# Two layer-norm weaves, one load and one block of values moved ahead in a fused attention and feed-forward kernel

## The chip, the core and the metric

The kernel runs on one core of one Trainium2 chip. The metric is the time of one execution on the device in microseconds; lower is better. The core has five engines with instruction streams of their own: TensorE (PE; its weight loads are PEld), VectorE (DVE), ScalarE (ACT), GpSimd (POOL) and SyncE (SP), which here issues nearly all DMA transfers.

## The reference

A block of a transformer with conditioned layer norms: an attention with a compressive memory in four segments, and then a bilinear feed-forward part. Sizes: 2048 rows, width 512, 32 heads of 16, segments of 512 rows, inner width 1376, all float32.

```
mod = silu(c) @ w_mod ; sa, ca, ga, sb, cb, gb = 6 rows of 512
h = layernorm(x) * (1 + ca) + sa
q, k, v = heads(h @ wq), heads(h @ wk), heads(h @ wv)
M, z = 0, 0
for s in range(4):                        # segments
    p = softmax(qs ks^T / 4 + mask)       # mask: -1e9 where key > query position
    a_dot = p vs
    a_mem = phi(qs) M / (phi(qs) z + 1e-6)       # phi(t) = t + 1 if t > 0 else exp(t)
    o_s = g * a_mem + (1 - g) * a_dot            # g = sigmoid(beta), one per head
    M, z = M + phi(ks)^T vs, z + sum(phi(ks))
x = x + ga * (o @ wo)
h = layernorm(x) * (1 + cb) + sb
out = x + gb * (((h @ w_gate) * (h @ w_up)) @ w_down)
```

The mask in full: `(ar[:, None] < ar[None, :]) * (-1e9)` over query and key positions.

## The kernel before

**Precision.** Dense products are made of three matmuls: operands are split into a high part (rounded to the fp32r format, names ending in H) and a low remainder (ending in L), and H·H, L·H and H·L are accumulated. Queries and keys are split into three bf16 parts and written to DRAM (`qd`, `kd`), from where `load(u)` reads them back into stacked tiles `qst`, `kst` (96 rows).

**Attention units.** A unit is one segment, one half of a head group: 4 heads. There are 4 segments x 4 head groups x 2 = 32 units. For a unit, five `q_step`s make scores with queries on the partitions; VectorE reduces each to a negated row maximum `nm` (the custom operation at L39, in place in the PSUM tile `q`, followed by a read of its accumulator). The score tiles have two PSUM banks, `lq0` and `lq1`. `n_step` transposes the maxima (`ntp`), rounds them to two bf16 rows (`nt`) and sends these with two small DMAs into rows 96 and 97 of `qst`. Five `k_step`s then make scores with keys on the partitions, maximum already taken off by those rows; ScalarE takes the exponential (`pt`, L289), GpSimd zeroes the masked part (L292). `av_step` multiplies with the values into `tb`, and `t_step` transposes back (`tr`) and scales into `orow`. `load` is L230, the `nt` DMAs L269.

**The loop.** The main loop runs over `v` from -2 to 32, each with five slots. In slot `slot` of turn `v` there are: one `q_step` of unit v+1 or v+2, in slot 1 the four `av_step`s of unit v-1, in slot 4 its `t_step`, then a portion of fill, and one `k_step` of unit v. TensorE's instructions stay in the order in which the program calls them (`MM` and `TP` chain each to the one before). VectorE's do as well from the loop on (`vec.eng = CV`). ScalarE's, GpSimd's and SyncE's instructions are ordered by a scheduler that plans with estimated times; `pin` ties some of them behind the TensorE instruction called last.

**The fill.** Everything else is written as generators. `fill_a` makes values (`a_v`), key and query projections (`a_kq`, PSUM tiles `kps`, `qps`), memory steps (`a_mem`: `mp`, `mz`, `up`) and the layer norms of segments 1 to 3 (`ln`, names beginning with `a`); `fill_b` makes output projections (`wo_op` transposes `op` and splits them into `oH`, `oL`; `wo_mm` multiplies into `wops`), the split of `wo` (`woH`, `woL`) and the norm `lnC` of the feed-forward part (`ctp`, `chf`, `chH`). Each yields the cost of what it has called (0.68 for three matmuls of 128x512, 0.45 for a group of transposes, 0.0 for steps with no TensorE work). `fill(share)` adds share x 5.5 to a credit and draws steps until it is used up; a yielded `False` ends the portion. The shares of the five slots are 0.25, 0, 0.25, 0.25, 0.25. What is left when the last unit is done is run at once, ahead of the feed-forward part, which then runs over four segments with TensorE alone in front.

**The layer norm.** `ln` yields 0.0 after each of four row statistics (`bn_stats` and `bn_aggr` on VectorE, tiles `ast`, `amv`), after the inverse deviation (two ScalarE and five GpSimd operations, `asd`, `ay`), and after each of four applications (`tensor_scalar` on VectorE, L39, on the row tiles `x`). Then come four groups of transposes (`atp`), each followed by a ScalarE scaling (`ahf`, L183), rounding (`ahH`) and a GpSimd remainder (`ahL`, L191). `weave(a, b, at)` runs generator `a` and draws one step of `b` behind those yields of `a` whose number is in `at`; a projection `a_kq` has four such yields. For segments 2 and 3 the norm is woven into the query projection of head group 2 and both projections of group 3; for segment 1 only into both of group 3. What is left of it runs unwoven ahead of the next segment (`yield from lns`).

**Before the loop.** The weights of a head group are loaded raw into a staging buffer (`staged`, tags from the list `stage`) and split by ScalarE and GpSimd. The tag `x` has four buffers; the rows of segment 0 use them first, then the raw weights of head groups 1, 2 and 3, and the rows of segment 1 (`xload`, L459) come behind these. Projections of head groups 0 and 1 and two of four value blocks of segment 0 are made ahead of the loop; two more blocks come as the first fill.

Of the kernel before, what the change touches and what calls it, by code (L numbers as in the profile page):

```python
# [8 lines left out]
F32 = mybir.dt.float32  # L9
# [8 lines left out]
P = 128  # L18
S, D, H, DH, NSEG, L, F = 2048, 512, 32, 16, 4, 512, 1376
# [38 lines left out]
def tile_kernel(ctx, tc, x, wq, wk_, wv, wo, beta, w_gate, w_up, w_down, c, w_mod, out):  # L58
# [4 lines left out]
    def open_pool(**kw):  # L63
        p = tc.tile_pool(**kw)
        return p, p.__enter__()
# [18 lines left out]
    def MM(*a, **k):  # L84
        return pe(nc.tensor.matmul(*a, **k))  # L85
# [12 lines left out]
    def pst(shape, tag, name, dt=F32):  # L98
        tg, n = TAGS[tag]
        return psp.tile(list(shape), dt, tag=tg, name=name, bufs=n)  # L100
# [105 lines left out]
    apool, ap = open_pool(name="ap", bufs=1)  # L206
# [20 lines left out]
    def load(u):  # L227
        s, g, j = u // 8, u // 2 % 4, u % 2
        for t, d in ((kst[u % NB], kd), (qst[u % NB], qd)):
            nc.sync.dma_start(t[0:96].rearrange("p h t -> p (h t)"),  # L230
                              d[s][g].rearrange("r (d h) t -> (r d) (h t)", h=HG)[:, j * HQ * L:(j + 1) * HQ * L])
# [3 lines left out]
    def q_step(u, i):  # L235

        Q, K = qst[u % NB], kst[u % NB]
        if i == 0:
            nms[u] = ap.tile([P, 16], F32, tag="nm", name=f"nm{u}", bufs=2)
        nm = nms[u]  # L240
        for b in range(2):
# [7 lines left out]
            for hh, qb in parts:  # L249
                n = (qb + 1) * P  # L250
                MM(qp[:, c:c + n], Q[0:96, hh, qb * P:(qb + 1) * P], K[0:96, hh, 0:n], start=True, stop=True)
                c += n
# [7 lines left out]
    def n_step(u):  # L260

        Q = qst[u % NB]
        tp = pst([16, P], "tb", f"ntp{u}", F32)
# [4 lines left out]
        for i in range(2):  # L268
            nc.sync.dma_start(Q[96 + i:97 + i].rearrange("p h (q t) -> p (h q) t", t=P), nt[:, i])  # L269

    def k_step(u, i):

        Q, K = qst[u % NB], kst[u % NB]
        kp = psp.tile([P, 2, 512], F32, tag="lk", name=f"k{u}_{i}", bufs=1)

        def mm(b, c, h, kb):
            MM(kp[:, b, c:c + L - kb * P], K[:, h, kb * P:(kb + 1) * P], Q[:, h, kb * P:], start=True, stop=True)

# [164 lines left out]
    papool, pa = open_pool(name="pa", bufs=2, reuse_waits="tile")  # L443
# [3 lines left out]
    def load_mod(i):  # L447
        r = []
        for k in range(KT):
            a = pa.tile([P, 512], F32, tag="x", name=f"wm{i}_{k}", bufs=4)  # L450
            nc.sync.dma_start(a, wm[:, k, i * D:(i + 1) * D])
            r.append(a)
        return r

    def xload(s):
        xt = []
        for t in range(4):
            a = pa.tile([P, D], F32, tag="x", name=f"x{s}_{t}", bufs=4)
            pin(nc.sync.dma_start(a, x[rows(s, t), :]))  # L459
            xt.append(a)  # L460
        return xt
# [37 lines left out]
    def mod_acc(r):  # L499
        for k in range(KT):  # L500
            pin(act.activation(r[k], r[k], AF.Identity, scale=s_c[:, k:k + 1]))
            if k > 0:
                nc.gpsimd.tensor_add(r[0], r[0], r[k])
            yield 0.0
# [44 lines left out]
    def a_ln(s):  # L549
        return ln(pa, pa, xts.pop(s), s, ca_c, sa_c, "a", ("h", 8, 2), s == 0)  # L550

    def weave(a, b, at):

        i = 0
        for w in a:
            yield w
            if w:
                for _ in range(at.count(i)):
                    w = next(b, None)
                    if w or w is False:  # L560
                        yield w
                i += 1

    wH, wL = {}, {}
    stage = [("ph", 3), ("ph", 3), ("ph", 3), ("mem", 1), ("pkr", 1), ("f", 2)] + [("x", 4)] * 6
    nst = [0]

    def staged(nm):
        tg, n = stage[nst[0] % len(stage)]
        nst[0] += 1  # L570
        return pa.tile([P, D], F32, tag=tg, name=f"wr{nm}", bufs=n)

    def load_g(nm, w, g):

        A, V = (CA if g == 0 else act), (CV if g == 0 and nm == "q" else nc.gpsimd)
        raw = staged(f"{nm}{g}")
        hi = wH[nm, g] = pa.tile([P, KT, P], F32R, name=f"w{nm}H{g}", bufs=1)
        lo = wL[nm, g] = pa.tile([P, KT, P], F32R, name=f"w{nm}L{g}", bufs=1)
        pin(nc.sync.dma_start(raw.rearrange("p (k c) -> p k c", c=P),
                              w.rearrange("(k p) n -> p k n", p=P)[:, :, g * P:(g + 1) * P]))  # L580
        yield
        hi, lo = (a.rearrange("p k (d h) -> p k h d", h=HG) for a in (hi, lo))
        raw = raw.rearrange("p (k h d) -> p k h d", k=KT, h=HG)
        pin(A.activation(hi, raw, AF.Copy))
        V.tensor_sub(lo, raw, hi.bitcast(F32))
        yield
# [14 lines left out]
    def a_v(s):  # L601
        hH, hL = hcur[0]
        for t in range(4):
            ps = bank(f"vps{s}_{t}")
            tt = slice(t * P, (t + 1) * P)
            n = 0
            for k in range(KT):
                for a, b in ((hH, wH), (hL, wH), (hH, wL)):
                    MM(ps, a[k][:, tt], b["v", k], start=n == 0, stop=n == 11)
                    n += 1  # L610
                    if n in (3, 6, 9):
                        yield 0.68
            act.activation(vt[s % 2][t][:, 0:H * VS].rearrange("p (h e) -> p h e", e=VS)[:, :, 0:DH],
                                 ps.rearrange("p (h e) -> p h e", e=DH), AF.Copy)
            yield 0.68
# [78 lines left out]
    def drain():  # L694
        while memq:
            w = mem_step()
            if w is not None:
                yield w
# [42 lines left out]
    def a_mod(i, a):  # L741

        if i == 2:
            bcast(a, gab, "gaps")
        elif i == 5:
            bcast(a, gbb, "gbps")
        else:
            cols(a, (sb_c, cb_c)[i - 3], f"mc{i}")
            if i == 4:
                vec.tensor_scalar_add(cb_c, cb_c, 1.0)  # L750
        yield 0.6
# [23 lines left out]
    def fill_a():  # L775
        for w in w2:
            next(w)
        yield from av
        memq.extend((a_mem(0, 0), a_mem(0, 1)))
        lns = None  # L780
        for s in range(NSEG):
            if s > 0:
                hcur[0] = yield from lns
                if s < 3:
                    r = load_mod(2 * s)
            for g in range(2 if s == 0 else 0, NG):
                ws = []
                if s == 0 and g < 3:
                    ws = [load_g(nm, w, g + 1) for nm, w in (("k", wk_), ("q", wq))]
                for w in ws:  # L790
                    next(w)
                K, Q = a_kq(s, g, "k"), a_kq(s, g, "q")
                if g >= 2 and s + 1 < NSEG:
                    if g == 2:
                        xts[s + 1] = xload(s + 1)
                        lns = a_ln(s + 1)
                        if s > 0:
                            Q = weave(Q, lns, (0, 1, 2, 3))
                    else:
                        K = weave(K, lns, (1,) if s > 0 else (0, 1, 2, 3))  # L800
                        Q = weave(Q, lns, (0, 1, 2, 3))
                if g == 1 and 0 < s < 3:
                    acc = mod_acc(r)
                    K, Q = weave(K, acc, (0, 2)), weave(Q, acc, (0, 2))
                if s == NSEG - 1 and g == NG - 1:
                    yield from Q
                    memq.append(a_mem(s, g))
                    yield from K
                    break
                yield from K  # L810
                for w in ws:
                    next(w)
                yield from Q
                if s > 0 and g == 0:
                    while vfree[0] < s:
                        yield None
                    if s < 3:
                        yield from weave(a_v(s), mod_acc(r), (1, 3, 5, 7))
                        yield from a_mod(2 * s, r[0])
                        r = load_mod(2 * s + 1)  # L820
                    else:
                        yield from a_v(s)
                        B["orl"] = wo_load(0, wpool)
                        B["raw"] = [wo_raw(k, wpool, "wor", 2) for k in (0, 1)]
                if g == 1 and 0 < s < 3:
                    yield from a_mod(2 * s + 1, r[0])
                memq.append(a_mem(s, g))
        for w in drain():
            yield w
            yield False  # L830
# [79 lines left out]
    av = a_v(0)  # L910
# [11 lines left out]
    flush()  # L922
    load(1)
    load(2)
    btag[:] = ["ms"]
    vec.eng = CV
    share = (0.25, 0.0, 0.25, 0.25, 0.25)
    for v in range(-2, NQ + 1):
        rate[0] = 5.5
        on, prev = 0 <= v < NQ, 0 <= v - 1 < NQ  # L930
        for slot in range(5):
            i = (slot + 3) % 5
# [53 lines left out]
    for s in range(NSEG):  # L986
# [30 lines left out]
        for i in range(NF):  # L1017
            if i + 1 < NF:
                gate_up(i + 1)
            n = ft[i][1]  # L1020
# [47 lines left out]
```

## Time and profile before

| | |
|---|---|
| median of 3 runs | 920.62 us (920.42 to 922.03) |
| the profiled execution | 918.26 us, span 916.5 us, mean granted TensorE clock 0.989 |
| TensorE busy | 874.2 us (95% of the span), 5083 matmuls |
| VectorE busy | 525.5 us (57%) |
| ScalarE busy | 408.4 us (45%) |
| GpSimd busy | 316.1 us (34%) |
| first score matmul of attention | 41.66 us |

The profile is of one execution. Busy shares are of the whole span; the loop of attention units fills it from about 42 to 527 us, the feed-forward part from 540 us on. The line of an instruction is that of the helper which recorded it: L85 is every matmul of `MM`, L88 every transpose of `TP`, L39 every operation that goes through a chain. So an instruction is told by its tile. A wait names the instruction that ended it, as inferred from semaphores.

### The profile page before, as it was taken

Reading aid. Unit: us, or ns where it says so; the run is one execution under the profiler, and the core shown is the slowest. Engines: PE = TensorE matmul, PEld = TensorE weight load, DVE = VectorE, ACT = ScalarE, POOL = GpSimd, SP = SyncE. Lnnn points to the kernel's source line nnn. Section 1 sums busy time; section 2 is a strip of 40 time slices with the busy share of each in tenths; the row PEclk is TensorE's granted clock in tenths of the full one; section 3 lists DMA queues with packets and bytes.
Section 4 is the critical chain, followed back from the end, with each engine's and each line's share of the span. In section 5 each row is a group of like instructions: output and inputs, shape, how many; then the busy total and the mean of one; then the engine's idle time right before and its main releaser. Section 6 shows DMA issues by size and latency. Waiting matters only on the chain.

```text
span 916.5 us, 14189 instructions
## 1 busy us (share of the span) xinstructions
PE 874.2 (95%) x5083; PEld 623.9 (68%) x5084; DVE 525.5 (57%) x1586; ACT 408.4 (45%) x603; POOL 316.1 (34%) x456
## 2 busy tenths in 40 slices
PE   8898999989999899998997999999999999999998
PEld 5665656656656566565655678887888788878886
DVE  8598778878789787696886326552133213321112
ACT  3667757787577865674546412231112111211111
POOL 4545536566465752665423406540000000000000
PEclk9999999999999999997999999999999999999999
DMA  7774545664455544568551433431101110100011
GB/s 230 223 214 145 156 127 153 194 204 146 135 165 168 177 146 135 177 200 290 163 171 61 134 129 106 113 95 58 46 1 47 46 47 0 46 18 29 1 46 46
DMA packets 86215, 109.81 MB, mean 120 GB/s; under 512 B 9504, under 2 KB 58656, under 8 KB 86144
## 3 DMA queue, kind: packets, MB, share of 16 engines
q1 hardware_dynamic: 86000, 108.89, 38.4%
q8 instruction: 40, 0.66, 0.3%
q14 instruction: 31, 0.25, 0.1%
q10 hardware_dynamic: 144, 0.02, 0.0%
HBM read 67.98 MB, written 40.63 MB: 119 GB/s over the span
## 4 chain that ended last, share of the span: by engine, by line
PE 77%; DVE 14%; ACT 4%; DMA 2%; issue 1%; POOL 1%; SPq 0%; DVEq 0%; ACTq 0%
PE gps L1004 13%; PE acc L1025 13%; PE ups L1004 13%; DVE q L39 7%; PE tb L85 7%; PE k L85 6%; PE q L85 5%; PE wops L85 4%; PE vps L85 3%; PE qps L85 3%; PE kps L85 3%; ACT pt L289 2%; DVE nm L39 1%; PE tr L88 1%; PE wups L85 1%
## 5 line engine op out<-in xcount | busy, mean ns | idle before, releaser
L39 DVE CUSTOM_DVE_ANT_0 q<-q,cmask 128x384 f32<-128x384 f32 (+3 forms) x512 | 245.9, 507 | 61.6 <-PE q L85 53.4
L289 ACT ACTIVATE pt<-k 128x1024 f32<-128x1024 f32 x160 | 163.7, 1023 | 75.4 <-PE k L85 72.3
L292 POOL TENSOR_SCALAR_AFFINE_SELECT pt<-pt 128x256 f32<-128x256 f32 (+1 forms) x224 | 100.3, 461 | 175.4 <-ACT pt L289 175.4
L1009 DVE TENSOR_TENSOR gs<-gs,ups 128x512 f32<-128x512 f32 (+1 forms) x44 | 30.2, 687 | 195.0 <-PE ups L1004 195.0
L85 PE MATMUL q<-kst,qst 96*128 96x384 bf16 (+3 forms) x512 | 103.5, 301 | 11.9 <-DVE nm L39 8.6
L85 PE MATMUL k<-qst,kst 98*128 98x384 bf16 (+3 forms) x512 | 98.4, 305 | 8.2 <-ACT pt L289 8.2
L1008 ACT ACTIVATE gs<-gps 128x512 f32<-128x512 f32 (+1 forms) x44 | 26.2, 598 | 147.0 <-PE gps L1004 147.0
L1012 ACT ACTIVATE mH<-gs 128x512 fp32r<-128x512 f32 (+1 forms) x44 | 27.8, 632 | 129.8 <-DVE gs L1009 126.3
L85 PE MATMUL tb<-pt,v 128*32 128x512 f32 (+3 forms) x1024 | 75.5, 436 | 0.0
L85 PEld LDWEIGHTS <-kst 98*128 98x128 bf16 x512 | 39.0, 99 | 50.7 <-issue 44.0
L39 DVE DVE_READ_ACCUMULATOR2_ANT nm<- 128x1 f32 x512 | 72.2, 141 | 0.0
L85 PEld LDWEIGHTS <-qst 96*128 96x128 bf16 x512 | 46.0, 98 | 36.6 <-issue 11.2
L1004 PE MATMUL gps<-chH,gL 128*128 128x512 f32 (+1 forms) x176 | 69.3, 394 | 0.0
L1004 PE MATMUL gps<-chH,gH 128*128 128x512 f32 (+1 forms) x176 | 69.3, 394 | 0.0
L1004 PE MATMUL ups<-chH,uH 128*128 128x512 f32 (+1 forms) x176 | 69.3, 394 | 0.0
L1025 PE MATMUL acc<-dH,mL 128*128 128x512 f32 (+1 forms) x176 | 69.3, 394 | 0.0
L1025 PE MATMUL acc<-dL,mH 128*128 128x512 f32 (+1 forms) x176 | 69.2, 393 | 0.0
L1004 PE MATMUL ups<-chL,uH 128*128 128x512 f32 (+1 forms) x176 | 69.2, 393 | 0.0
L1004 PE MATMUL gps<-chL,gH 128*128 128x512 f32 (+1 forms) x176 | 69.2, 393 | 0.0
L1004 PE MATMUL ups<-chH,uL 128*128 128x512 f32 (+1 forms) x176 | 69.2, 393 | 0.0
L1025 PE MATMUL acc<-dH,mH 128*128 128x512 f32 (+1 forms) x176 | 65.0, 395 | 0.0
L85 PEld LDWEIGHTS tb<-pt,v 128*32 128x32 f32 x1024 | 28.7, 109 | 38.6 <-issue 35.0
(213 smaller groups left out, 1655.8 us busy)
## 6 DMA issues: line engine op xcount, KB each, us to landing
kst<-kd SPq DMA_DIRECT2D x32, 384.0 KB, 4.5
qst<-qd SPq DMA_DIRECT2D x32, 384.0 KB, 5.2
wm<-in_w_mod_dram SPq DMA_DIRECT2D x24, 256.0 KB, 5.3
kd<-k SPq DMA_DIRECT2D x16, 384.0 KB, 4.3
qd<-q SPq DMA_DIRECT2D x16, 384.0 KB, 2.9
x<-in_x_dram SPq DMA_DIRECT2D x16, 256.0 KB, 4.3
kd<-k SPq DMA_DIRECT2D x16, 256.0 KB, 3.4
qd<-q SPq DMA_DIRECT2D x16, 256.0 KB, 3.8
```

The costliest lines, as they stand in the source:

```text
L39: i = getattr(self.eng, name)(*a, **k)
L85: return pe(nc.tensor.matmul(*a, **k))
L88: return pe(nc.tensor.transpose(*a))
L289: act.activation(pt, kp, AF.Exp, scale=0.25)
L292: sels[u, i] = nc.gpsimd.affine_select(w, w, pattern=[[0, w.shape[1]], [1, P]], compare_op=ALU.is_ge, fill=0.0, base=0, channel_multiplier=-1)
L1004: nc.tensor.matmul(ps[0:n], a[:, k, 0:n], b[k], start=j == 0, stop=j == 11)
L1008: act.activation(gs[0:n], pss[0][0:n], AF.Copy)
L1009: vec.tensor_mul(gs[0:n], gs[0:n], pss[1][0:n])
L1012: act.activation(mH[0:n], gs[0:n], AF.Copy)
L1025: nc.tensor.matmul(acc[t], a[0:n, t * P:(t + 1) * P], b[0:n, :], start=i == 0 and j == 0, stop=i == NF - 1 and j == 2)
```

## The change

Three edits. First, `stage`: the last two of twelve raw weights (head group 3, key and query) no longer take buffers of tag `x`, but one of `mem` and one of `memb`, a tag of another pool that attention uses from segment 1 on. The rows of segment 1, loaded where head group 2 starts, then take buffers whose former weights are those of head groups 1 and 2. Second, the weave: segment 1's norm is treated as the others', its statistics woven into the query projection of head group 2; and for all three segments the deviation and four applications go behind yields 0, 1 and 3 of the key projection and 0 and 2 of the query projection of head group 3 (before: yield 1 of the key projection and 0 to 3 of the query projection for segments 2 and 3, and for segment 1 all four yields of both, statistics included). Third, four more steps of `av`, that is one more value block, are drawn ahead of the loop.

```
-    stage = [("ph", 3), ("ph", 3), ("ph", 3), ("mem", 1), ("pkr", 1), ("f", 2)] + [("x", 4)] * 6
+    stage = [("ph", 3), ("ph", 3), ("ph", 3), ("mem", 1), ("pkr", 1), ("f", 2)] + [("x", 4)] * 4 + [("mem", 1), ("memb", 2)]
...
-        return pa.tile([P, D], F32, tag=tg, name=f"wr{nm}", bufs=n)
+        return (ap if tg == "memb" else pa).tile([P, D], F32, tag=tg, name=f"wr{nm}", bufs=n)
...
                     if g == 2:
                         xts[s + 1] = xload(s + 1)
                         lns = a_ln(s + 1)
-                        if s > 0:
-                            Q = weave(Q, lns, (0, 1, 2, 3))
+                        Q = weave(Q, lns, (0, 1, 2, 3))
                     else:
-                        K = weave(K, lns, (1,) if s > 0 else (0, 1, 2, 3))
-                        Q = weave(Q, lns, (0, 1, 2, 3))
+                        K = weave(K, lns, (0, 1, 3))
+                        Q = weave(Q, lns, (0, 2))
...
     flush()
     load(1)
     load(2)
+    for i in range(4):
+        next(av)
     btag[:] = ["ms"]
     vec.eng = CV
```

## The prediction

> **What bounds the kernel now.** I read the page's busy times first, then TensorE's waits, then the granted clock by stage, and last the timelines at the places that the change touches. A wait has its total, count and longest; a stretch the busy time of TensorE, its weight loads, VectorE, ScalarE and GpSimd, then the granted clock, the DMA share and GB/s; a row of a timeline its start, its length and, in brackets, the idle time ahead of it.
>
> ```profile
> span 916.5 us, 14189 instructions
> PE 874.2 (95%) x5083; PEld 623.9 (68%) x5084; DVE 525.5 (57%) x1586; ACT 408.4 (45%) x603; POOL 316.1 (34%) x456
> PE q L85 <- DVE nm L39: 8.6, 24, 0.5
> PE op L88 <- DVE oL L39: 3.3, 3, 1.6
> PE atp L88 <- DVE x L39: 2.7, 2, 1.7
> PE q L85 <- DMA qst<-qd: 2.4, 1, 2.4
> 60.00:80.00 20.00, 18.37 (x125) 11.41 (x123) 17.72 (x65) 13.34 (x20) 10.46 (x20) 1.00 0.42 142
> 80.00:100.00 20.00, 17.55 (x121) 11.82 (x122) 14.01 (x48) 14.42 (x21) 10.93 (x15) 0.91 0.42 133
> 420.00:440.00 20.00, 16.89 (x93) 11.01 (x92) 13.78 (x38) 8.30 (x13) 8.08 (x10) 0.74 0.88 289
> 500.00:520.00 20.00, 18.64 (x115) 13.06 (x115) 7.72 (x16) 11.04 (x15) 10.44 (x16) 0.91 0.40 127
> ```
>
> TensorE is busy for 874.2 of 916.5 us, and its order is written out by hand, so the time is its work, plus 42 us in which it stands idle, plus what it loses at a lower clock. The change adds and removes no arithmetic. It can only win from idle time and clock. Granted clocks of 0.91, 0.74 and 0.91 of full over 20 us mean 1.8, 5.2 and 1.8 us lost to the clock. Two of the waits are aimed at: the one on the first queries' transfer (2.4 us) and the one on the norm of segment 1 (2.7 us).
>
> The profiled execution took 918.26 us (the span and 1.76 us around it); the median of the runs is 920.62. I take the sum as a difference and set it against the median.
>
> **Term 1, the third block of values.**
>
> ```profile
> 36.98 0.40 PE L85 MATMUL vps<-wvH,ahH 128*128 128x512 f32 x1
> 38.84 0.40 PE L85 MATMUL vps<-wvL,ahH 128*128 128x512 f32 x1
> 41.66 0.60 PE L85 MATMUL q<-kst,qst 96*128 96x512 bf16 x2 [2.42 <-DMA qst<-qd]
> ```
>
> Nine value matmuls start between 36.98 and 38.84, one each 0.233 us, and then TensorE waits 2.42 us for the queries. In the order of the two programs, twelve more of them now stand ahead of the first score matmul (three that end block 2, nine of block 3): 12 x 0.233 = 2.80 us. They end at 39.07 + 2.80 = 41.87, 0.21 us after the queries land. So 2.80 us of work goes into a 2.42 us hole, and the scores start 0.21 us late: -2.6. This counts only if the lead lasts. The projections are filled between attention steps by a credit, and I compared the two orders step by step: the changed one stays ahead by 0.9 to 5 us of fill, mostly 2.8, up to the last unit. It never comes to stand at the places where the fill must wait for a finished segment. So the 2.8 us are missing from the projection matmuls that are left when attention ends, which run there with nothing beside them. Bounds: -2.8, and 0 if the fill that is gone later had covered a wait.
>
> **Term 2, the norm of segment 1, woven sooner.**
>
> ```profile
> 49.85 0.43 DVE L39 CUSTOM_DVE_ANT_0 q<-q,cmask 128x256 f32<-128x256 f32 x1
> 57.88 0.57 DVE L39 CUSTOM_DVE_ANT_0 q<-q,cmask 128x384 f32<-128x384 f32 x1 [0.23 <-PE q L85]
> 61.34 0.43 DVE L39 CUSTOM_DVE_ANT_0 q<-q,cmask 128x256 f32<-128x256 f32 x1
> 65.85 0.69 DVE L39 BATCH_NORM_STATS2 ast<-x 128x6 f32<-128x512 f32 x1
> 66.67 0.66 DVE L39 BATCH_NORM_STATS2 ast<-x 128x6 f32<-128x512 f32 x1
> 70.22 0.18 DVE L39 BATCH_NORM_AGGREGATE amv<-ast 128x2 f32<-128x6 f32 x1
> 74.21 0.20 POOL L167 TENSOR_TENSOR ay<-ay,ayb 128x4 f32<-128x4 f32 x1
> 78.02 0.54 DVE L39 TENSOR_SCALAR x<-x,amv,ay 128x512 f32<-128x512 f32 x1
> 81.35 0.33 PE L88 MATMUL atp<-ident,x 128*128 128x128 f32 x1 [1.74 <-DVE x L39]
> 82.64 0.78 PE L88 MATMUL atp<-ident,x 128*128 128x128 f32 x2 [0.97 <-DVE x L39]
> 89.56 2.36 PE L85 MATMUL tb<-pt,v 128*32 128x512 f32 x32
> ```
>
> Before, the four statistics (one each 0.82 us, from 65.85 to 66.67) stand in unit 2, and the four applications end just ahead of the transposes, which wait 1.74 + 0.97 us. In the new order, VectorE's chain has all four statistics between the fourth reduction step of unit 0 and the fourth of unit 1, and the first application ahead of the last step of unit 1. There VectorE is back to back: from 49.85 to 61.7 (61.34 and its last step) it waits 0.23 us once, and hardly else. So those two units end later by 4 x 0.82 + 0.5 (one application, from 78.02) and by a wait: the inverse deviation was ready 4.0 us after the last statistic (70.4 to 74.4), and now only one step and a small product, about 2 us, lie between; some 0.9 us of that stays, as ScalarE and GpSimd have less ahead of them. Less 0.2 of idle: +4.5. The queue behind the waiting application is the reductions, and behind them TensorE's score matmuls, which share two banks. In return unit 2 loses its statistics, the transposes no longer wait (-2.7), three of TensorE's 24 waits for a reduction (8.6 / 24 = 0.36 us on the mean, 1.1 in all) go, and the dip of the clock that follows the wait for the transposes (1.8 us in 80 to 100) has no cause left: -5.6. I expect a part of it to come back as other waits and take 0 for the whole; bounds +4.5 (nothing regained) and -1.1. At 0, the value product of unit 1 stands again at 89.6.
>
> The rows of segment 1 come sooner because the weights of the fourth head group no longer take their buffers. On SP's queue the two weights and four rows, six transfers, now stand ahead of the second head group's last writes and of the loads of units 2 and 3. The cover:
>
> ```profile
> qst<-qd SPq DMA_DIRECT2D x32, 384.0 KB, 5.2
> 49.80 0.42 SPq L230 DMA_DIRECT2D qst<-qd  x1
> ```
>
> The last of these loads was issued at 49.80 and lands in the median 5.2 us later, at 55.0; unit 2 reads its own only from 61.7 on. That is 6.7 us in hand against six issues of some 0.4 us and their bytes, so I cost this at 0; if the cover were gone, unit 2 would wait for what is left of a transfer, up to 5.2 us.
>
> ```profile
> 198.79 1.04 PE L88 MATMUL atp<-ident,x 128*128 128x128 f32 x8
> 203.61 2.50 POOL L191 TENSOR_TENSOR ahL<-ahf,ahH 128x512 fp32r<-128x512 f32 x2
> 500.82 1.11 PE L88 MATMUL op<-ident,orl 128*128 128x128 f32 x4 [1.72 <-ACT chf L183]
> ```
>
> **Term 3, the norms of segments 2 and 3.** They already stood one block sooner; their last two applications move by a block at most. But the fill is now cut differently: all twelve matmuls of the first key projection follow in the very next slot after the last two transposes. Before, a value product of 2.3 us and three smaller portions lay between. From the last transposes (198.79) to the last low half (203.61 + 2.50) passed 7.3 us. A slot is 2.9 us (from 41.66 to 500.82 there are 161). Now TensorE asks for that half one slot and nine matmuls (2.1 us) later, after 5.0 us, and could wait up to 2.3 us. The old order paid waits there also, on the probabilities; I take +1.0 for each of the two segments: +2.0, bounds 0 and +4.6.
>
> **Term 4, the first output projection.**
>
> ```profile
> 411.44 2.36 PE L85 MATMUL tb<-pt,v 128*32 128x512 f32 x32
> 416.99 1.04 PE L88 MATMUL op<-ident,orl 128*128 128x128 f32 x8
> 420.80 0.66 PE L88 MATMUL op<-ident,orl 128*128 128x128 f32 x4 [0.67 <-DVE oL L39]
> 423.10 1.11 PE L88 MATMUL op<-ident,orl 128*128 128x128 f32 x4 [1.64 <-DVE oL L39]
> 424.38 0.63 ACT L771 ACTIVATE woH<-wor 128x512 fp32r<-128x512 f32 x1 [2.23 <-POOL wor L759]
> 426.72 0.79 PE L85 MATMUL wops<-woH,oH 128*128 128x512 f32 x1 [0.80 <-DVE oL L39]
> 427.74 0.63 PE L85 MATMUL wops<-woL,oH 128*128 128x512 f32 x1
> 432.64 0.40 PE L85 MATMUL wops<-woL,oH 128*128 128x512 f32 x1
> ```
>
> This is where the lead does most. Before, the four groups of transposes stand in two neighbouring slots with only short score matmuls between, and TensorE waits 0.67 + 1.64 + 0.80 us for what ScalarE and VectorE make of them and of the weights (ScalarE itself waits 2.23 us). The clock then falls to half: a matmul takes 0.63 us at 427.74 and 0.40 again at 432.64, and the 20 us lose 5.2 us, some 0.4 of it inside a wait. In the new order the groups fall into slots 0 and 1 of unit 25, with a value product (2.36 us, as at 411.44) between the pairs and one slot without fill ahead of the projection: about 3.3 us more attention work inside the same chain. I take 3.0 us of waiting and 4.8 us of clock as gone: -7.8. The second output projection is now cut as this one was, without room: +1.0. Bounds: -8, and 0 if the clock falls all the same.
>
> [...]
>
> **Term 5, the norm for the feed-forward part.**
>
> ```profile
> 489.27 0.33 PE L88 MATMUL ctp<-ident,x 128*128 128x128 f32 x1 [0.63 <-DVE x L39]
> 491.28 0.66 PE L88 MATMUL ctp<-ident,x 128*128 128x128 f32 x4 [0.87 <-ACT chf L183]
> 497.95 0.60 PE L85 MATMUL k<-qst,kst 98*128 98x384 bf16 x4 [1.39 <-ACT pt L289]
> ```
>
> These transposes move two to three slots forward, into units that still have score matmuls. ScalarE's chain stays as long, so most of the 4.6 us of waiting (these three and the 1.72 at 500.82) stays; with the 1.8 us of clock in 500 to 520 I take -1.5, bounds -5 and +1.
>
> **The sum.** -2.6 + 0 + 2.0 - 7.8 + 1.0 - 1.5 = -8.9 us; 920.6 - 8.9 = 911.7.
>
> **The rivals.**
> First, the late dip stays. Terms 1 to 3 and 5 with the small part of term 4: the waits at 420 shrink by a microsecond or two, but what idle time is left still falls into one stretch, and 5 us of clock stay lost. For it: a dip shows in three stretches only, though there are 24 waits for reductions alone, so which bunch of waits trips it is a close thing. That gives -2.6 + 0 + 2.0 - 1.5 = -2.1, so 918.5. [...]
> Second, the opening becomes VectorE's. The statistics lie in two units where VectorE has no room, and what they cost (+4.5) isn't regained, since units 2 and 3 run at VectorE's pace as well (17.72 of 20 us busy from 60 to 80); the wait of the first application for the deviation leaves TensorE idle near 62 to 65 and a dip of 1.8 us follows. With term 1 that is -2.6 + 4.5 + 1.8 = +3.7, and 924.3 where the late stretch gives nothing. It decides if unit 2 starts over 4 us later than 61.7 and the value product of unit 1 isn't back at 89.6. Against it: VectorE drops to 14.01 of 20 from 80 on.
> Third, the lead does nothing: the fill that ran ahead had covered waits, the moved work leaves equal holes, 920.6. For it, that attention is paced by three engines in turn; against it, that only 42 us of TensorE's span are idle at all.
>
> **Chances.** Forecast 0.52 (its own range 907 to 916), late dip stays 0.22, nothing 0.10, VectorE's opening 0.16. A measurement here can tell about 0.2%, 1.8 us, from no change. Faster: 0.50 + 0.16 of the second case, 0.66; same: 0.01 + 0.06 + 0.08 + 0.02 = 0.17; slower: 0.14 + 0.02 + 0.01 = 0.17. The range reaches from 907 to 921.5: it leaves out some 0.05 of the forecast below and most of the slow case above.
>
> **What would show it.** Term 1: the wait for the queries' transfer is gone from TensorE's list, and the first score matmul starts near 41.9. Term 2: no wait of the transposes for the norm, a clock of 1.00 from 80 to 100, statistics before 61 and unit 1's last reduction near 66 in place of 61.7. Term 3: waits of the key projection for low halves at the start of segments 2 and 3, about 1 us each. Term 4: a clock near 1.00 between 405 and 440 and waits for the transposed outputs under 1 us. The forecast is wrong if the clock's loss turns up again at 0.74 there, or if the value product of unit 1 starts well after 89.6, or if a new dip appears in the opening or where segments 2 and 3 begin.

## The result and the profile after

The changed kernel takes 929.1 us in the median (925.59 to 930.51), the kernel before 920.62 us (917.81 to 924.5) beside it: 1.0077 times as long, 95% interval 1.0055 to 1.0100. By the ratio it is 7.1 us slower, by the two medians 8.5. The prediction was 911.7 us, and its range ended at 921.5. The profiled execution took 928.15 us.

The head of the page and some of TensorE's waits (total, count, longest):

```profile
span 926.4 us, 14197 instructions
PE 875.9 (95%) x5084; PEld 623.5 (67%) x5084; DVE 521.9 (56%) x1586; ACT 408.1 (44%) x603; POOL 315.0 (34%) x456
PE q L85 <- DVE nm L39: 10.5, 27, 0.8
PE k L85 <- ACT pt L289: 5.9, 11, 1.6
PE op L88 <- DVE oL L39: 5.0, 3, 1.9
PE mz L85 <- DVE orow L39: 2.6, 2, 1.5
PE kps L85 <- POOL ahL L191: 2.4, 5, 0.9
PE atp L88 <- DVE x L39: 2.3, 2, 2.1
PE kps L85 <- ACT ahf L183: 1.3, 2, 1.1
```

TensorE's busy time nearly stays (875.9 against 874.2 us); the span grows by 9.9 us, so most of the loss, 8.2 us, is idle time. The wait for the queries' transfer (2.4 us before) is gone, and the one for the probabilities `pt` fell from 8.2 to 5.9. The list has grown elsewhere: `op` waits 5.0 us in place of 3.3, the wait for the row maxima, the reductions, went from 8.6 to 10.5, `mz` behind `orow` from 0.7 to 2.6, and `kps` now waits 3.7 us for the halves of the norm, where it waited 0.6 before. By stretch (busy times, then granted clock, DMA share, GB/s):

```profile
60.00:80.00 20.00, 15.90 (x97) 10.71 (x99) 17.64 (x62) 11.95 (x19) 10.34 (x17) 1.00 0.40 112
80.00:100.00 20.00, 19.22 (x158) 12.40 (x152) 13.41 (x53) 16.36 (x24) 12.24 (x16) 1.00 0.56 181
420.00:440.00 20.00, 14.79 (x88) 9.12 (x87) 11.62 (x38) 8.93 (x13) 8.96 (x13) 0.74 0.93 313
500.00:520.00 20.00, 16.70 (x107) 9.98 (x110) 10.69 (x30) 11.20 (x16) 9.52 (x13) 0.91 0.12 43
520.00:540.00 20.00, 18.18 (x132) 12.08 (x125) 5.72 (x12) 8.27 (x11) 6.77 (x11) 0.91 0.46 145
```

In this trace the dip from 80 to 100 is gone, as term 2 had it; other traces of the same opening have new ones (below). The dip from 420 to 440 is there in full, and TensorE is busy for 14.79 us of it in place of 16.89. One from 520 to 540 is new. From TensorE's timeline, the opening and the start of segment 2:

```profile
43.55 0.61 PE L85 MATMUL q<-kst,qst 96*128 96x512 bf16 x2
53.24 1.19 PE L85 MATMUL mz<-v,pkr 128*128 128x136 f32 x8 [1.06 <-ACT pkr L710]
78.72 0.33 PE L88 MATMUL atp<-ident,x 128*128 128x128 f32 x1 [2.10 <-DVE x L39]
189.42 1.16 PE L85 MATMUL mz<-v,pkr 128*128 128x136 f32 x8 [1.15 <-DVE orow L39]
202.71 0.50 PE L85 MATMUL kps<-ahH,wkH 128*128 128x512 f32 x1 [1.06 <-ACT ahf L183]
205.55 0.50 PE L85 MATMUL kps<-ahL,wkH 128*128 128x512 f32 x1 [0.72 <-POOL ahL L191]
```

The first score matmul has no wait. The whole opening of this execution is late: the first value matmul starts at 27.59 in place of 25.93. Counted from there, the scores start 0.2 us later than before, as term 1 had it. The memory product `mz` waits for ScalarE's copy of `pkr` near the start of the loop, and at 189 until VectorE has made `orow` from `tr`: it now stands one portion of fill behind the transposes `tr`, and the two tiles share a PSUM buffer (tag `sm`). The key projections wait for both halves of the new norm. And around the first output projection, TensorE, then ScalarE; the last line is ScalarE's first `oH` in the kernel before:

```profile
419.25 1.04 PE L88 MATMUL op<-ident,orl 128*128 128x128 f32 x8
421.08 2.36 PE L85 MATMUL tb<-pt,v 128*32 128x512 f32 x32
425.38 0.66 PE L88 MATMUL op<-ident,orl 128*128 128x128 f32 x4 [1.93 <-DVE oL L39]
427.68 1.12 PE L88 MATMUL op<-ident,orl 128*128 128x128 f32 x4 [1.64 <-DVE oL L39]
428.58 1.06 PE L85 MATMUL k<-qst,kst 98*128 98x512 bf16 x2
423.51 0.60 ACT L318 ACTIVATE tsb<-tb 128x512 f32<-128x512 f32 x1 [1.73 <-PE tb L85]
424.01 0.59 ACT L399 ACTIVATE oH<-op 128x512 fp32r<-128x512 f32 x1
429.31 0.63 ACT L771 ACTIVATE woH<-wor 128x512 fp32r<-128x512 f32 x1 [2.58 <-POOL wor L759]
...
419.43 0.59 ACT L399 ACTIVATE oH<-op 128x512 fp32r<-128x512 f32 x1
```

The value product stands between the pairs, as predicted. But ScalarE's order has its eviction `tsb` ahead of `oH`. So the first `oH` of the pair transposed at 419.25 starts at 424.01, 4.8 us later and after the value product; before, it started at 419.43, 2.4 us behind the transposes of 416.99. The next two groups wait 1.93 + 1.64 us. This is read from the trace; no run changes ScalarE's order alone.

### The profile page after: what moved, and what is told of

Same layout as the page of the kernel before. It is cut to its first block, busy times and chain, and to the rows that moved or that the text cites. A ratio compares the mean times of both kernels' runs of the same rounds, so it can differ in the third digit from the quotient of the medians.

```text
span 926.4 us, 14197 instructions
## 1 busy us (share of the span) xinstructions
PE 875.9 (95%) x5084; PEld 623.5 (67%) x5084; DVE 521.9 (56%) x1586; ACT 408.1 (44%) x603; POOL 315.0 (34%) x456
## 4 chain that ended last, share of the span: by engine, by line
PE 71%; DVE 12%; DMA 5%; ACT 5%; POOL 3%; issue 2%; SPq 1%; DVEq 0%; ACTq 0%; POOLq 0%
PE gps L1005 13%; PE acc L1026 13%; PE ups L1005 13%; PE tb L85 6%; DVE q L39 5%; PE k L85 5%; PE q L85 5%; PE wops L85 4%; PE vps L85 4%; PE qps L85 2%; ACT pt L289 2%; PE kps L85 2%; POOL ahL L191 1%; DVE x L39 1%; PE tr L88 1%
## 5 line engine op out<-in xcount | busy, mean ns | idle before, releaser
L39 DVE CUSTOM_DVE_ANT_0 q<-q,cmask 128x384 f32<-128x384 f32 (+3 forms) x512 | 245.9, 508 | 74.1 <-PE q L85 66.2
L85 PE MATMUL q<-kst,qst 96*128 96x384 bf16 (+3 forms) x512 | 103.6, 302 | 11.6 <-DVE nm L39 10.5
```

The lines of the kernel that those rows point to most:

```text
L39: i = getattr(self.eng, name)(*a, **k)
```

## The experiments

In all of them "lead" means fill done ahead on TensorE: the third block puts twelve value matmuls (2.8 us) ahead of the loop, so that every later piece of fill moves to an earlier place. A lead is "paid back" by taking its cost off the credit, so that the fill pauses until it stands where it stood before. Gains and losses in microseconds are the ratio's difference from 1 times 920.6. Where two of them are subtracted, the uncertainty of both goes into the difference. Each trace is one execution.

**The parts alone.** The third block alone, added to the kernel before:

```
     load(2)
+    for i in range(4):
+        next(av)
```

> Kernel before with the third block of values alone ahead of the loop (old weave, old staging). Theory A, the lead cuts the fill badly: the order on TensorE is that of the changed kernel, so nearly all of the 8.5 us is here, 925 to 930. Theory B, the norm in the opening is what costs: the block alone gains what it was meant to, 917 to 919. Both expect the wait of 2.4 us for the first queries to be gone.

Measured: 932.44 us, 1.0129 (1.0101 to 1.0157). The block by itself costs 11.9 us, more than the whole change and more than theory A's 925 to 930. Its waits include what I had laid to the new weave:

```profile
PE atp L88 <- DVE x L39: 4.8, 2, 3.0
PE op L88 <- DVE oL L39: 4.6, 3, 1.9
PE mz L85 <- DVE orow L39: 2.7, 2, 1.5
PE kps L85 <- POOL ahL L191: 2.3, 5, 0.9
```

The old weave gives the same waits for the low halves (2.3 us) and at `mz` as the new one: they come from the lead. The leads from turns 4 and 8 below, which have no block, wait 2.3 and 2.4 us for the low halves too.

The changed kernel without that block (its four lines out):

> The changed kernel without the third block (new weave, new staging). Theory A: the order on TensorE is that of before, so 918 to 922. Theory B: 924 to 929, with reduction waits in the first two units.

Measured: 923.44 us, 1.0018 (1.0001 to 1.0035): +1.7. This lies between the two expectations. Most of the loss is gone with the block, so theory B, the norm in the opening as the main cause, falls.

The block alone again, with its lead paid back at once:

```
-    credit = [0.0]
+    credit = [-4 * 0.68]
```

> The third block alone, but its cost of 4 x 0.68 is taken off the credit of the fill, so that from the fourth unit-slot on the order on TensorE is that of before. Theory A: no bad cut, so 918 to 921; the gain of 2.4 us is mostly lost again, since the first two units then have less fill and wait for VectorE. Theory B: the same as the block alone, within 1 us.

Measured: 922.16 us, 1.0011 (0.9994 to 1.0028), a little above theory A's range. Without the lead the loss of 11.9 us is gone to within the interval, so it hangs on the lead and not on the block as such; but nothing is gained by the filled wait either.

**Repairs of single places.** The changed kernel with an empty slot ahead of the first key projection of segments 2 and 3 (`yield False` behind the norm, for s > 1):

> The changed kernel with one portion of fill ended between the norm and the first key projection of segments 2 and 3, so that the projection starts a slot later. Theory A with the norms of segments 2 and 3 as the place: 924 to 926, the waits for the low halves (2.4 us in all) and for the scaling (1.3) gone. If the slot only moves the idle time: 928 to 930.

Measured: 926.64 us, 1.0069 (1.0043 to 1.0095), between the two expectations. The waits at the start of segment 2 go (`kps` for the halves 2.1 us, now 0), but three units there take 49.4 us in place of 48.5: the reductions' wait grew from 2.2 to 3.2 us, and a clock of 0.91 appears. By the ratios (1.0069 against 1.0077) 0.7 us are gained, which the intervals don't resolve.

The changed kernel, with the transposes of the output projections cut to one head group a slot, and the same edit on the kernel before:

```
-            if g % 2 == 1:
-                yield False
+            yield False
```

> The changed kernel, with the transposes of the output projections cut into one head group a slot. Theory A (as above; in the changed kernel the value product stands between the pairs on ScalarE's queue): waits for the transposed outputs under 1 us in place of 3.6, 920 to 925 against 929 for the changed kernel. Rival (they only move): 927 to 930.

> The kernel before, with the transposes of the output projections cut into one head group a slot in place of two. Theory A (the waits at 420 us come from two groups in one slot, whose chain over ScalarE and VectorE takes longer than the slot; the dip follows the bunch of waits): the 3.1 us of waits and most of the 5 us of clock go, 912 to 917. Rival (the wait that ends last there is ScalarE's for the weights, which GpSimd scales; groups moved apart only move it): 919 to 922, clock still near 0.74 in that stretch.

Measured: 927.58 us, 1.0084 (1.0051 to 1.0117) from the changed kernel, as the rival had it and not theory A; 922.26 us, 1.0012 (0.9993 to 1.0031) from the kernel before. The second is the direct test of term 4's premise. The wait for the probabilities in the kernel before, then this run's waits and its stretch:

```profile
PE k L85 <- ACT pt L289: 8.2, 12, 1.4
...
PE q L85 <- DVE nm L39: 14.2, 32, 1.7
PE k L85 <- ACT pt L289: 9.8, 16, 1.3
420.00:440.00 20.00, 16.51 (x107) 10.42 (x106) 13.76 (x46) 9.55 (x15) 10.52 (x13) 0.91 0.87 266
```

The wait of `op` for `oL` (3.3 us before) is off the list and the clock goes from 0.74 to 0.91: all that term 4 wanted. Of these 3.4 us of clock, 1.7 may be chance: in the eight traces that keep the old order of these transposes and the same 3.3 us of waits, the dip lasts 10.2 us at half clock in three and 6.8 us in five; here it lasts 3.4. Yet the reductions' wait rises from 8.6 to 14.2 us and the one for the probabilities from 8.2 to 9.8, and the time stays. The trace shows it in the place itself: from the transposes `ntp` of unit 26 to those of unit 30 it takes 66.2 us, and 66.0 in the kernel before, with the same fill done in between. The idle time of TensorE there changes its name. That the units go at the pace of the chain over VectorE and ScalarE is my reading of this; no run makes that chain shorter. My rival (groups moved apart only move the wait) held for the time, though not for the clock.

The changed kernel, with the statistics of segment 1 taken over 64 of 512 columns (another norm):

> The changed kernel, with the four statistics of segment 1's norm taken over 64 of 512 columns, so that VectorE has some 2.4 us less to do in units 0 and 1; the order is that of the changed kernel, the norm is another. Theory V (VectorE sets the pace of the opening, and the norm moved there costs what its statistics take): 925 to 927. Theory A (the lead's bad slots, VectorE's statistics only fill what it waits anyway): 928 to 929.5.

Measured: 926.86 us, 1.0069 (1.0049 to 1.0089). The median lies in theory V's range, but 1.9 us less on VectorE (four statistics of 0.22 us in place of 0.68) bring 0.7 us by the ratios, well within the interval. It doesn't tell the two apart.

**Where the lead costs.** First, the changed kernel with the lead paid back later, at the turn named (`if v == 8: credit[0] -= 4 * 0.68` at the head of the loop's turn; 15 and 23 likewise):

> The changed kernel, with the lead of 2.7 us of fill paid back at turn 8 of the attention loop: from unit 9 on TensorE's order is that of the kernel before. Theory A (what is lost is lost at a few places where the lead shifts a dependent group: norm of segment 2 about +5, of segment 3 +3, output projections and tail +3, opening +1 to 2): only the opening and the first part of segment 2's norm stay, 921 to 923.5. Rival C (the lead loses a little in every unit, evenly): 29% of the 8.5 us stay, about 923. Rival D (all of it comes from the output projections and the tail): 920 to 921.

> The changed kernel, with the lead paid back at turn 15: from unit 16 on the order is that of the kernel before. Theory A: opening and the norm of segment 2 stay (+1.5 and +5), 925 to 927. Rival C (evenly): half stays, about 925. Rival D (all from the output projections and the tail): 920 to 922.

> The changed kernel, with the lead paid back at turn 23, so that only the output projections and the tail are in the order of before. Theory A: opening, norms of segments 2 and 3 stay, the 3 us of the late part go or come back by chance of the clock, 926 to 929. Rival C (evenly): three quarters stay, about 927. Rival D (all from the output projections and the tail): 920 to 922.

Measured: 928.57 us, 1.0081 (1.0065 to 1.0097); 927.88, 1.0065 (1.0050 to 1.0081); 930.56, 1.0094 (1.0077 to 1.0111). None comes back to before, and every expectation missed, theory A's and its rivals'. All three keep the opening with the lead and the new weave of the other norms, and paying back may itself cost (it is a shift of the size of the lag below), so this series doesn't tell the place. Giving the lead to the kernel before is cleaner (`credit[0] += 4 * 0.68` at turn 23, 4, 8 or 12, and nothing else):

> The kernel before, with a lead of 2.7 us of fill given at turn 23 of the attention loop and nothing else changed: the order of the output projections, the feed-forward norm and the tail is that of the changed kernel. The prediction's term 4 and 5 (value product between the pairs of transposes gives room): 912 to 914. Theory A (the value product stands ahead of the chain on ScalarE's queue, so the waits and the dip stay, and the tail gets new waits): 922 to 925. Rival C (evenly over the units): 922 to 923.

> The kernel before, with a lead of 2.7 us of fill given at turn 4 of the attention loop, after the opening, and nothing else changed. Theory A (dependent groups land in bad slots at the norm of segment 2, +3.5 to 5; segment 3 about 0, the late part 0 to 3): 924 to 927. Theory V (the loss of the block is made in the opening, where VectorE has no room): 921 to 923.

> The kernel before, with a lead of 2.7 us of fill given at turn 8 of the attention loop and nothing else changed. The lead from turn 4 cost about 7 us, that from turn 23 none. Theory A (the norm of segment 2, units 9 to 11, is where it costs): as much as from turn 4, 925 to 928. Rival C (evenly over units 4 to 22): 6 of the 7 us, 925 to 926, so that only the run from turn 12 tells the two apart.

> The kernel before, with the lead given at turn 12, behind the norm of segment 2. Theory A: 920 to 922. Rival C (evenly): 11 of 19 units left, 924 to 925.

| lead from turn | us | ratio (95%) | difference |
|---|---|---|---|
| 4 | 927.88 | 1.0076 (1.0047 to 1.0105) | +7.0 |
| 8 | 929.35 | 1.0086 (1.0058 to 1.0113) | +7.9 |
| 12 | 924.89 | 1.0037 (1.0023 to 1.0052) | +3.4 |
| 23 | 922.40 | 1.0001 (0.9987 to 1.0014) | +0.1 |

From turn 23 on, the transposes, the value product between the pairs and the norm for the feed-forward part stand as in the changed kernel: terms 4 and 5 by themselves, -8.3 us predicted, +0.1 measured. The losses from turn 4 and turn 8 are a little above what theory A had. Between the leads from turns 8 and 12 lie 4.5 us (7.9 - 3.4), the start of segment 2. What the block alone costs more than a lead from turn 4 (11.9 - 7.0, 4.9 us) would arise in the opening; these differences have wide intervals. The 3.4 us from turn 12 on speak for the rival that the lead costs along the way, which the 7.9 us from turn 8 had not borne out. No single theory fits all four.

Traces narrow two of the places down. For the start of segment 2, the transposes `ntp` of units 8 and 12, in the kernel before and then in the one with the lead from turn 8:

```profile
164.25 0.27 PE L88 MATMUL ntp<-ident,nm 128*16 128x128 f32 x1
...
221.67 0.27 PE L88 MATMUL ntp<-ident,nm 128*16 128x128 f32 x1
```

```profile
167.93 0.27 PE L88 MATMUL ntp<-ident,nm 128*16 128x128 f32 x1
...
231.68 0.28 PE L88 MATMUL ntp<-ident,nm 128*16 128x128 f32 x1
```

57.4 us between them become 63.8. Of the 6.3 us (10.0 - 3.7), 2.8 are the fill that was done ahead, and 3.5 are lost. The eight traces that come to this place with the lead already taken, and without the empty slot, take 4.4 to 4.7 us longer for it than the kernel before (4.4 in the block alone, 4.7 in the changed kernel); six others that have the order of before there take at most 0.01 us longer.

For the opening, the first units of the loop, the granted clock tells most. The third column adds up what is lost from 40 to 100 us to a clock below 1.00; the last is the time from the first value matmul to the `ntp` of unit 3, as a difference from the kernel before:

| order of the opening | traces | lost to the clock, us | up to unit 3, us |
|---|---|---|---|
| as before | kernel before, and with it the leads from turns 4, 8, 12 and 23, the lag, one group a slot | 1.7 to 3.4 | -0.2 to +1.7 |
| norm of segment 1 sooner, no lead | without the block; the norm alone; the norm with the block paid back at once | 0 in all three | -1.9 to -0.8 |
| as changed, with the lead | changed kernel; the same paid back at turn 8 | 0 in both | +1.3, +0.8 |
| as changed, with the lead | changed kernel with the empty slot, paid back at turns 15 and 23, one group a slot, old weave of segments 2 and 3 | 5.1 to 6.8 | +4.7 to +5.8 |

In the last two rows 2.8 us of the last column are fill done ahead. So with the lead, one and the same opening has two dips of the clock in five traces of seven, which is a sign of a wrong forecast that the prediction named; the changed kernel's own profile happens to be one of the two without. Why the clock dips there in some executions only is open.

Where the 3.4 us of the lead from turn 12 go stays open. In its trace unit 23 comes 5.7 us late, of which 2.9 stand before the first value matmul and 2.8 are the lead itself, so that the loss shows only behind it. But the trace of the lead from turn 23 also loses 3.6 us there against the one trace of the kernel before, and its median loses nothing.

The same size the other way, a lag from turn 4 on (`credit[0] -= 4 * 0.68`):

> The kernel before, with the fill 2.7 us behind from turn 4 of the attention loop on. Theory A (any shift takes dependent groups out of the places in which they wait least): 923 to 927. Rival L (a lead costs because what depends on other engines is asked for too early, so a lag gives): 916 to 920.

Measured: 936.93 us, 1.0171 (1.0147 to 1.0195): +15.7. So it is not that a lead asks too early: a shift to either side costs, and this one more than twice the most that I expected. The waits are of the same kinds:

```profile
PE op L88 <- DVE oL L39: 5.0, 3, 1.9
PE atp L88 <- DVE x L39: 4.1, 3, 1.7
PE mz L85 <- DVE orow L39: 2.6, 2, 1.4
```

**The norm of segment 1 alone.** The changed kernel without the block and with the old weave of segments 2 and 3:

```
-                        K = weave(K, lns, (0, 1, 3))
-                        Q = weave(Q, lns, (0, 2))
+                        K = weave(K, lns, (1,) if s > 0 else (0, 1, 3))
+                        Q = weave(Q, lns, (0, 1, 2, 3) if s > 0 else (0, 2))
```

> The changed kernel without the third block of values and with the norms of segments 2 and 3 woven as before: what is left is the norm of segment 1 woven sooner, with its rows. The prediction's term 2 (nothing): 920 to 921. Theory V (VectorE's opening, +3.7): 923 to 925. If the whole 1.6 us of the run without the block are its own, 922 to 922.5; if they belong to term 3, 920 to 921.

Measured: 919.01 us, 0.9969 (0.9955 to 0.9982): a gain of 2.9 us, which no expectation had. By this, the new weave of segments 2 and 3 costs 1.0018 - 0.9969, 4.5 us, where there is no lead. Two of its waits and three stretches:

```profile
PE k L85 <- DMA qst<-nt: 2.4, 1, 2.4
PE atp L88 <- DVE x L39: 1.4, 1, 1.4
20.00:40.00 20.00, 20.00 (x81) 16.42 (x80) 11.72 (x20) 15.78 (x23) 7.49 (x5) 0.87 0.56 171
80.00:100.00 20.00, 18.08 (x136) 12.01 (x134) 13.40 (x51) 15.00 (x21) 11.35 (x16) 1.00 0.46 149
420.00:440.00 20.00, 16.93 (x98) 10.76 (x96) 13.90 (x43) 9.46 (x14) 9.14 (x12) 0.83 0.90 289
```

The transposes still wait 1.4 us, and a transfer of 2.4 us takes the place of the rest; but the dip from 80 to 100 is gone, as in the two other traces of this opening without a lead (second row of the table). The dip from 420 to 440 is smaller in this execution, though the order there is that of before.

The same edit on the changed kernel, which keeps the block:

> The changed kernel, with the norms of segments 2 and 3 woven as before: the third block and the norm of segment 1 are left. If the parts add (block alone 1.0129, norm of segment 1 alone 0.9969): 1.010, about 930. If the new weave costs its 1.5 to 4.5 us in the changed kernel also: 925 to 927.5. If the new weave gains there, since the lead has moved the slots: 930 to 932.

Measured: 930.38 us, 1.0088 (1.0066 to 1.0110). The parts add within the intervals: block (1.0129 - 1) and norm (0.9969 - 1) give 1.0098. Beside the lead, the new weave of segments 2 and 3 is worth -1.0 us (1.0077 - 1.0088), not told from nothing.

And the norm of segment 1 sooner, with the block and its lead paid back at once:

> The norm of segment 1 woven sooner (0.9969) with the third block, whose lead is paid back before unit 0 (1.0011). If the parts add: 0.998, 918.5 to 920. Theory A (the block fills a real hole, but unit 0 goes at VectorE's pace, so nothing is gained by it): 918 to 920. The prediction's term 1 (2.6 us gained, and a lead paid back at once has no bad slots): 915.5 to 917.

Measured: 917.97 us, 0.9963 (0.9948 to 0.9978), the fastest version, 3.4 us under the kernel before. The block adds 0.6 us to the norm's gain, which isn't told from nothing; term 1's 2.6 us are not there.

## Why the prediction was wrong

Taken apart one after the other, the change comes to this: norm of segment 1 -2.9, third block with its lead 1.0088 - 0.9969 = +11.0, new weave of segments 2 and 3 beside it -1.0. These add up to the 1.0077 because each is a difference of neighbouring runs. The prediction had -8.9. The step that failed and cost most is in terms 1, 4 and 5: that a lead of 2.8 us of fill is harmless where it comes to no limit, and useful where it spreads a crowded chain. Together they had -10.9 us; the block with its lead measured +11.0.

- **Term 1 (-2.6; measured about 0 without the lead).** The wait was filled, as predicted: no wait at 43.55. What failed is "this counts only if the lead lasts", taken as a gain with a worst case of 0. The lead lasts, and costs. Paid back at once, the block brings +1.0 and -0.6 us in two settings. That the fill which is missing later had covered waits of the first units is what I take from it; no run takes those waits away by themselves. The 0 was in the bounds as the end of the range; a loss was not. I had compared the orders for how far ahead the fill runs, and not for which matmuls each slot now holds.
- **Term 2 (0, bounds +4.5 to -1.1; measured -2.9).** Its mechanism held: alone, the `ntp` of unit 1 comes 3.1 us late (5.95 less the 2.89 that stand before the first value matmul), unit 3 has it back, and the dip is gone (a granted clock of 1.00 from 80 to 100, 0.91 before). The term was mis-sized: the gain of the clock was worked out at 1.8 us and then given up for "other waits". The three traces without a lead lose nothing to the clock there, and the seven of the old opening 1.7 to 3.4 us, so the clock can be most of the 2.9.
- **Term 3 (+2.0; measured +4.5 without the lead, -1.0 beside it).** The sign was right where the weave stands alone, but not the wait that the term names: without the block no matmul waits for a low half. There the trace falls back by 1.1 us between units 9 and 10 and by 2.6 between units 17 and 19, where the reductions wait 1.7 us once and one dip of the clock follows (1.7 us lost at the least, see the last point). In the changed kernel the waits for the low halves did come, 2.4 us in all, but the block with the old weave has them as well.
- **Term 4 (-7.8 + 1.0) and term 5 (-1.5); measured +0.1 together.** Two steps failed. The value product was counted as room inside the chain; its eviction is itself ahead of `oH` on ScalarE's queue, and the waits grew (1.93 + 1.64 against 0.67 + 1.64). And where an edit did take the waits and a part of the dip away (the kernel before with one group a slot), the time stayed: the waits there weren't worth their length.
- **The rivals.** "The late dip stays" was right in its sign of the dip (0.74 again) and wrong in the time, because it kept term 1. "VectorE's opening" ended on the right side, 924.3, by another mechanism; that it came nearest was luck: without the block there is no such loss. No rival had the lead doing harm.
- **The length of the late dip.** In slices of 1 us the granted clock falls to 0.50 and no lower. Between 30 and 900 us, every stretch at this half clock in the twenty traces lasts 3.4, 6.8 or 10.2 us, which costs 1.7, 3.4 or 5.1 us. The late one lasts 10.2 us in the kernel before (from 422 to 432) and in the changed kernel (from 426 to 436): term 4 had its size about right, and what failed is that it would go. What sets a dip off stays open. TensorE's longest wait around 420 is 1.64 us before and 1.93 us after. In the changed kernel the clock falls within 5.1 us in which only transposes stand, between the value product that ends at 423.44 and the score matmul at 428.58. But in the changed kernel with the old weave of segments 2 and 3 the clock falls at 55, behind waits of 0.8 us and less, with no such stretch.

## What to carry to other kernels

Where a stream of filler work is dealt out by a credit beside a chain of dependent steps, a block moved ahead shifts every later piece of filler; list what each later slot holds before and after, and price the shift as a loss of unknown size, not as zero. A wait of the busiest engine need not be worth its length: here a run without 3.3 us of waits and with 1.7 to 3.4 us less clock loss was no faster (1.0012), which I read as another engine's chain ending just behind the wait. Fill a hole with work that is paid back at once, and test each part of a change alone.

## What the runs showed of the hardware

Not expected: the first 40 us of one and the same order ran at different granted clocks in different profiles. The kernel before, and then the same kernel with a lead that starts only at turn 12:

```profile
20.00:40.00 20.00, 18.48 (x75) 13.77 (x75) 12.40 (x17) 16.56 (x25) 9.80 (x7) 1.00 0.65 194
20.00:40.00 20.00, 20.00 (x81) 16.48 (x81) 13.41 (x19) 15.80 (x23) 7.04 (x5) 0.87 0.55 171
```

In the second the first value matmul starts 2.9 us later, long before the lead begins. The norm of segment 1 alone has the same 2.9 us; its profiled span is 916.7 us against 916.5, though its median is lower by 2.5 us. Two single traces are to be compared from behind such a stretch on. The late dip varies in the same way: 6.8 us at half clock in five traces and 10.2 us in three, 1.7 us apart in cost, where the order on TensorE and the waits for `oL` are the same.
